# A recurrent attention and a maxout layer in one kernel: units of four batches with four tokens a partition, 32-row tiles and a tabled order in place of units of two batches and a stepped loop

## The chip, the core and the metric

The kernel runs on one core of one Trainium2 chip. The engines of the core run side by side, each with a queue of its own that it works off in order: TensorE (PE; its loads of weights, PEld, are listed apart), VectorE (DVE), ScalarE (ACT), GpSimd (POOL), and SyncE (SP), which here only issues DMA transfers. Matmul results go to PSUM, eight banks of 2 KB a partition; GpSimd does not read PSUM in this kernel. The metric is the device time of one execution in microseconds, lower is better; the median of the runs is given.

## The reference

Two stages in float32. The first is a recurrence with a decay for each channel (4 batches, 8 heads, 768 tokens, head size 48); the second a maxout layer over all 3072 tokens (384 to 1024 and back), whose input row holds the 8 heads of one token side by side.

```python
for t in range(S):
    cur = np.einsum('bhd,bhe->bhde', u[None] * kt, vt)
    y[:, :, t] = np.einsum('bhd,bhde->bhe', rt, state + cur)
    state = wt[:, :, :, None] * state + np.einsum('bhd,bhe->bhde', kt, vt)
...
h1 = x @ w1
h2 = x @ w2
g = np.maximum(h1, h2)
return (g @ w_out).astype(np.float32)
```

## The kernel before

The recurrence is done in chunks of 128 tokens. With P the running product of the decays inside a chunk, the score of token t for an earlier token s is r·P(before t) times k/P(through s); the scores are masked to earlier tokens and multiplied with v ("intra"). The state that comes in adds r·P times S ("carry"), and the token itself adds v times the sum of u·r·k ("bonus"). The state after the chunk is (S + sum of k/P times v) times the whole chunk's P.

*Tiles.* A unit is one chunk of two batches: 256 tokens, 12 units. 64 partitions hold a batch, each with two neighbouring tokens (`i` = 0, 1). `load` (L71) issues eight DMAs a unit (w, k, r, v for two batches), each with pieces of 384 B.

*A unit's work.* `logw` (L167): Ln on ScalarE, the pair's sum on GpSimd. `cumsum` (L194): an fp32 matmul with a triangular matrix gives the sum of the logarithms of all partitions before; VectorE adds the tokens' own. `exps` (L206): Exp of these sums and of their negatives, and a DMA on ScalarE's queue writes the last row to DRAM, from where `decay_load` (L218) fetches it again in the layout of the state. `scale_rk` (L227) multiplies r and k; `transp` (L233) turns them on TensorE (16 transposes) and VectorE copies them out of PSUM. `kv` (L253, 64x64 tiles of the array), `scores` (L284, 48x64 tiles; VectorE masks in one multiply each), `y_inter` (L300: the bonus rows placed by a selection matrix, L308, and the carry, L315), `y_intra` (L319, 64x128 tiles). ScalarE copies y out, `xt` (L335) turns it.

*The maxout layer.* max(h1, h2) = ((h1 + h2) + |h1 - h2|) / 2. So `gate` (L344) makes x @ (w1 - w2), in 24 matmuls of 256 columns, and ScalarE takes Abs; `outp` (L359) adds x @ wc to |.| @ (w_out / 2), where wc = (w1 + w2) @ w_out / 2 is folded once, in `weights` (L143).

*The order.* It is the program's order. `step(a, t, m)` (L376) interleaves three units: the preparation of `a`, the recurrence of `t`, the maxout layer of `m`. Two units go ahead, then comes `weights()`, then ten steps with all three. `load(n + 2)` stands ahead of a step. Loads have four buffers; output DMAs (one for 128 tokens) stand on the same SP queue, between the loads. A DMA waits until the eighth before it has landed, so at most eight are in flight.

Of the kernel before, what the change touches and what calls it, by code (L numbers as in the profile page):

```python
# [33 lines left out]

def _body(tc, r, k, v, w, u, moe_w1, moe_w2, moe_w_out, out):
# [3 lines left out]
    C = 128  # L39
    Q = C // 2  # L40
    NC = S // C
# [6 lines left out]
    NU = NC * B // 2  # L48
# [4 lines left out]
    ldp = tc.alloc_tile_pool(name="ld", bufs=4)  # L53
    wk = tc.alloc_tile_pool(name="wk", bufs=2)
    drp = tc.alloc_tile_pool(name="dr", bufs=3, space=bass.MemoryType.DRAM)
    ps = tc.alloc_tile_pool(name="ps", bufs=1, space=bass.MemoryType.PSUM)

    def wt_(shape, dt, tag, bufs=None):
        return wk.tile(shape, dt, tag=tag, name=tag, bufs=bufs)

    def pt_(shape, dt, tag, bufs=1):
        return ps.tile(shape, dt, tag=tag, name=tag, bufs=bufs)

    def unit(n):
        return n // 2, (n % 2) * 2

    L = {}

    def load(n):  # L71
        c, b0 = unit(n)
        d = {}
        for name, src in (("w", w), ("k", k), ("r", r), ("v", v)):
            t = ldp.tile([P, H, 2, D], F32, tag="l" + name, name="l" + name)
            for b in range(2):
                nc.sync.dma_start(  # L77
                    out=t[b * Q:(b + 1) * Q].rearrange("p h i d -> p h (i d)"),
                    in_=src[b0 + b, :, c * C:(c + 1) * C, :].rearrange(
                        "h (p i) d -> p h (i d)", i=2))  # L80
            d[name] = t
        L[n] = d

    load(0)
    u_b = const.tile([P, HD], F32)
    nc.sync.dma_start(out=u_b, in_=u.rearrange("h d -> (h d)").partition_broadcast(P))
    load(1)
    w1f = const.tile([P, KO, d_ff], F32)
    w2f = const.tile([P, KO, d_ff], F32)
    wof = const.tile([P, FO, HD], F32)  # L90
    nc.sync.dma_start(out=w1f, in_=moe_w1.rearrange("(o p) n -> p o n", p=P))
    nc.sync.dma_start(out=w2f, in_=moe_w2.rearrange("(o p) n -> p o n", p=P))
    nc.sync.dma_start(out=wof, in_=moe_w_out.rearrange("(o p) n -> p o n", p=P))
    load(2)


    triS = const.tile([P, P], F32)
    make_upper_triangular(nc, triS, val=1.0, diag=False)
    triI = const.tile([P, P], F32)
    make_upper_triangular(nc, triI, val=1.0, diag=True)  # L100
    tri2 = const.tile([P, P], F32)
    nc.gpsimd.memset(tri2, 0.0)
    ident = const.tile([P, P], BF16)
    make_identity(nc, ident)
    mask = const.tile([P, 2, 2, Q], F32)
    sel = const.tile([P, 2, 2, Q], BF16)
    nc.gpsimd.memset(sel, 0.0)
    for b in range(2):
        q = slice(b * Q, (b + 1) * Q)
        nc.gpsimd.tensor_copy(tri2[q, q], triS[q, q])  # L110
        for i in range(2):
            nc.gpsimd.tensor_copy(sel[q, i, i, :], ident[q, q])
            for i2 in range(2):
                nc.gpsimd.tensor_copy(mask[q, i, i2, :],
                                      (triI if (i, i2) == (0, 1) else triS)[q, q])

    NRK = 2
    rkn_b = []
    for i in range(NRK):
        t = const.tile([P, 2, 2, H, DP], BF16, name=f"rkn{i}")  # L120
        nc.vector.memset(t, 0.0)
        rkn_b.append(t)
    MZ = [const.tile([P, 2, H, DP], F32, name=f"mz{i}") for i in range(2)]
    for t in MZ:
        nc.gpsimd.memset(t, 0.0)

    S_f = [const.tile([P, 2, NP, D], F32, name=f"Sf{g}") for g in range(2)]
    T_f = [const.tile([P, 2, NP, D], F32, name=f"Tf{g}") for g in range(2)]
    S_b = [const.tile([P, 2, NP, 2 * D], BF16, name=f"Sb{g}") for g in range(2)]
    for g in range(2):  # L130
        nc.vector.memset(S_f[g], 0.0)
        nc.vector.memset(S_b[g], 0.0)
    WL = [const.tile([P, 2, NP], F32, name=f"WL{i}") for i in range(2)]
    for t in WL:
        nc.vector.memset(t, 0.0)

    wd_sb = const.tile([P, KO, d_ff], BF16)
    ws_sb = const.tile([P, KO, d_ff], BF16)
    wo_sb = const.tile([P, FO, HD], BF16)
    wsT_sb = const.tile([P, FO, HD], BF16)  # L140
    wc_sb = const.tile([P, KO, HD], BF16)

    def weights():  # L143
        for ko in range(KO):
            nc.vector.tensor_sub(wd_sb[:, ko, :], w1f[:, ko, :], w2f[:, ko, :])
            nc.vector.tensor_add(ws_sb[:, ko, :], w1f[:, ko, :], w2f[:, ko, :])
        nc.scalar.mul(wo_sb, wof, 0.5)
        for ko in range(KO):
            tp = pt_([P, FO, P], BF16, "tr")
            for fo in range(FO):  # L150
                nc.tensor.transpose(tp[:, fo, :], ws_sb[:, ko, fo * P:(fo + 1) * P], ident)
            nc.vector.tensor_copy(
                wsT_sb.rearrange("p f (k c) -> p k f c", k=KO)[:, ko, :, :], tp)
        for ko in range(KO):
            wc_p = pt_([P, HD], F32, "go", 2)
            for fo in range(FO):
                nc.tensor.matmul(wc_p, wsT_sb[:, fo, ko * P:(ko + 1) * P],
                                 wo_sb[:, fo, :], start=(fo == 0), stop=(fo == FO - 1))
            nc.scalar.copy(wc_sb[:, ko, :], wc_p)


    U = {}

    def byi(t):
        return t.rearrange("p h i d -> p i h d")

    def logw(n):  # L167
        s = U[n] = {}
        s["lw"] = lw = wt_([P, H, 2, D], F32, "lw")
        nc.scalar.activation(lw, L[n]["w"], AF.Ln)  # L170
        s["lp"] = lp = wt_([P, H, D], F32, "lp")
        nc.gpsimd.tensor_add(lp, lw[:, :, 0, :], lw[:, :, 1, :])  # L172

    def bonus_mul(n):
        s = U[n]
        s["vb"] = vb = wt_([P, H, 2, D], BF16, "vb", 3)
        nc.gpsimd.tensor_copy(vb, L[n]["v"])
        s["rku"] = rku = wt_([P, H, 2, D], F32, "rku", 1)
        nc.gpsimd.tensor_mul(rku, L[n]["r"], L[n]["k"])  # L179
        nc.gpsimd.tensor_mul(  # L180
            byi(rku), byi(rku),
            u_b.rearrange("p (h d) -> p h d", h=H).unsqueeze(1).to_broadcast([P, 2, H, D]))

    def bonus_sum(n):
        s = U[n]
        dg = wt_([P, H, 2, 1], F32, "dg")
        nc.vector.reduce_sum(dg, s["rku"], axis=AX.X)  # L187
        s["vd"] = vd = wt_([P, 2, H, D], BF16, "vd", 3)
        nc.gpsimd.tensor_mul(byi_inv(vd), L[n]["v"], dg.to_broadcast([P, H, 2, D]))  # L189

    def byi_inv(t):
        return t.rearrange("p i h d -> p h i d")

    def cumsum(n):  # L194
        s = U[n]
        lw, lp = s["lw"], s["lp"]
        ex = pt_([P, HD], F32, "ex")
        nc.tensor.matmul(ex, tri2, lp.rearrange("p h d -> p (h d)"))  # L198
        s["A"] = A = wt_([P, 2, H, D], F32, "A")
        s["mz"] = mz = MZ[n % 2]  # L200
        exh = ex.rearrange("p (h d) -> p h d", h=H)
        nc.scalar.activation(A[:, 0], exh, AF.Exp)  # L202
        nc.vector.tensor_add(mz[:, 0, :, 0:D], exh, lw[:, :, 0, :])  # L203
        nc.vector.tensor_add(mz[:, 1, :, 0:D], exh, lp)

    def exps(n):  # L206
        s = U[n]
        mz = s["mz"]
        nc.scalar.activation(s["A"][:, 1], mz[:, 0, :, 0:D], AF.Exp)  # L209
        s["iA"] = iA = wt_([P, 2, H, D], F32, "iA", 1)  # L210
        nc.scalar.activation(iA, mz[:, :, :, 0:D], AF.Exp, scale=-1.0)
        c, b0 = unit(n)
        if c == NC - 1:
            return
        s["row"] = row = drp.tile([2, H * DP], F32, tag="row", name="row")
        nc.scalar.dma_start(out=row, in_=mz[Q - 1::Q, 1].rearrange("b h d -> b (h d)"))

    def decay_load(n):  # L218
        c, b0 = unit(n)
        if c == NC - 1:  # L220
            return
        s = U[n]
        s["WL"] = wl = WL[n % 2]
        nc.scalar.dma_start(out=wl.rearrange("d b p -> d (b p)"),
                            in_=s["row"].rearrange("b (p x) -> x (b p)", x=P))

    def scale_rk(n):  # L227
        s = U[n]
        s["rkn"] = rkn = rkn_b[n % NRK]
        nc.vector.tensor_mul(rkn[:, 0, :, :, 0:D], byi(L[n]["r"]), s["A"])  # L230
        nc.vector.tensor_mul(rkn[:, 1, :, :, 0:D], byi(L[n]["k"]), s["iA"])  # L231

    def transp(n, x):  # L233
        s = U[n]
        tp = pt_([P, NP, 2, 2, Q], BF16, "tr")
        for i in range(2):
# [8 lines left out]
    def decay_exp(n):  # L245
        c, b0 = unit(n)
        if c == NC - 1:
            return
# [127 lines left out]
    def step(a, t, m, ahead=True):  # L376
# [10 lines left out]
        if T: kv(t)  # L387
# [64 lines left out]
```

## Time and profile before

| what | us |
|---|---|
| median of 3 runs (226.53 to 227.88) | 227.76 |
| span of the profiled execution | 226.8 |
| TensorE busy | 159.0 |
| VectorE busy | 114.1 |
| GpSimd busy | 113.6 |
| ScalarE busy | 91.7 |
| first gate matmul | 55.9 |
| start of the last output copy on ScalarE | 216.45 |

The profiled execution is known by its span, from its first to its last instruction; the median of the other runs is 0.96 us above that. "Busy" is the time in which at least one instruction of the engine was running; matmuls are pipelined, so their busy time holds latencies. "SPq" is time in which SP issues DMAs, or waits to issue them. A row of a timeline gives the start, the time from the first start to the last end of a group of like instructions, the engine, the line, the tiles and the count.

### The profile page before, as it was taken

What the parts mean: (1) busy time and instruction counts of PE and PEld (TensorE: products, weight loads), DVE (VectorE), ACT (ScalarE), POOL (GpSimd) and SP (SyncE); (2) the same over time, 40 slices, a digit from 0 to 9 for tenths busy, and PEclk for the clock granted to TensorE, in tenths of its full rate; (3) what the DMA queues carried; (4) which work ended last, traced back from release to release, by engine and by line L of the source; (5) the groups of instructions that cost most, each with busy time, mean ns of one, the idle gap of its engine ahead of it and who ended that gap; (6) DMA issues with size and microseconds to landing.
All of it is one profiled execution on the core that took longest, in us unless ns stands there. A gap on an engine that the chain in (4) does not pass through costs nothing.

```text
span 226.8 us, 5085 instructions
## 1 busy us (share of the span) xinstructions
PE 159.0 (70%) x2104; PEld 104.3 (46%) x2104; DVE 114.1 (50%) x135; ACT 91.7 (40%) x159; POOL 113.6 (50%) x118
## 2 busy tenths in 40 slices
PE   0216557195799848898839898378888398988910
PEld 0014444153576634666615656236556156665600
DVE  5166878710969490185840785802858405660000
ACT  2233113303765613464433556035644347344500
POOL 8494750004788828638549179086295494300000
PEclk9999999999999995899976999959999679999975
DMA  6979999990296439539584485385385811111110
GB/s 128 211 113 217 406 356 134 198 152 0 66 150 129 104 104 172 133 76 151 141 163 104 100 169 117 101 158 132 85 143 146 177 49 50 53 52 31 48 42 35
DMA packets 66254, 28.91 MB, mean 127 GB/s; under 512 B 61220, under 2 KB 65444, under 8 KB 66232
## 3 DMA queue, kind: packets, MB, share of 16 engines
q1 hardware_dynamic: 55792, 28.51, 55.0%
q10 hardware_dynamic: 10440, 0.08, 2.7%
q8 instruction: 16, 0.26, 0.5%
q14 instruction: 6, 0.05, 0.1%
HBM read 23.83 MB, written 4.76 MB: 126 GB/s over the span
## 4 chain that ended last, share of the span: by engine, by line
DMA 20%; PE 16%; SPq 8%; ACT 5%; issue 2%; DVE 1%; POOL 0%; ACTq 0%; DVEq 0%
DMA lw<-in_w_dram 20%; PE go L367 6%; SPq L77 6%; PE go L352 3%; PE go L364 3%; SPq L373 2%; ACT gT L356 2%; PE sc L293 1%; PE y L328 1%; ACT xT L342 1%; ACT osb L370 1%; ACT lw L170 1%; DVE kT L243 1%; PE y L315 1%; PE y L308 1%
## 5 line engine op out<-in xcount | busy, mean ns | idle before, releaser
L172 POOL TENSOR_TENSOR lp<-lw 128x384 f32<-128x384 f32 x12 | 12.3, 1022 | 60.5 <-ACT lw L170 39.5
L367 PE MATMUL go<-wo_sb,gT 128*128 128x384 bf16 x192 | 40.8, 362 | 0.0
L352 PE MATMUL go<-xT,wd_sb 128*128 128x256 bf16 x288 | 37.2, 273 | 2.5 <-ACT xT L342 1.5
L296 DVE TENSOR_TENSOR M<-sc,mask 128x1024 bf16<-128x1024 f32 x24 | 29.3, 1221 | 8.4 <-PE sc L293 8.4
L364 PE MATMUL go<-wc_sb,xT 128*128 128x384 bf16 x72 | 19.0, 381 | 18.7 <-ACT gT L356 18.7
L352 PEld LDWEIGHTS <-wd_sb 128*128 128x128 bf16 x288 | 26.9, 98 | 10.3 <-issue 5.5
L243 DVE COPY rT<-tr 128x1024 bf16<-128x1024 bf16 x12 | 8.3, 688 | 45.8 <-PE tr L238 45.8
L356 ACT ACTIVATE gT<-go 128x512 bf16<-128x512 f32 x48 | 27.3, 588 | 5.6 <-PE go L352 5.4
L370 ACT COPY osb<-go 128x384 f32<-128x384 f32 x24 | 11.5, 478 | 43.3 <-PE go L367 43.3
L367 PEld LDWEIGHTS <-gT 128*128 128x128 bf16 x192 | 20.7, 108 | 16.7 <-issue 6.7
L198 PE MATMUL ex<-lp,tri 128*128 128x384 f32 x24 | 12.1, 592 | 19.5 <-POOL lp L172 14.8
L180 POOL TENSOR_TENSOR rku<-rku,u_b 128x768 f32<-128x768 f32 x12 | 22.4, 1863 | 0.9
L179 POOL TENSOR_TENSOR rku<-lr,lk 128x768 f32<-128x768 f32 x12 | 22.4, 1868 | 0.0
L189 POOL TENSOR_TENSOR vd<-lv,dg 128x768 bf16<-128x768 f32 x12 | 17.7, 1474 | 9.1 <-DVE dg L187 8.3
L170 ACT ACTIVATE lw<-lw 128x768 f32<-128x768 f32 x12 | 10.1, 842 | 29.2 <-DMA lw<-in_w_dram 29.2
L203 DVE TENSOR_TENSOR mz<-ex,lw 128x384 f32<-128x384 f32 x12 | 6.7, 557 | 27.9 <-ACT A L202 27.9
L238 PE MATMUL tr<-ident,rkn 128*128 128x128 bf16 x192 | 16.3, 234 | 4.3 <-DVE rkn L230 3.0
L364 PEld LDWEIGHTS <-xT 128*128 128x128 bf16 x72 | 6.5, 105 | 23.0 <-issue 21.0
L238 PEld LDWEIGHTS <-rkn 128*128 128x128 bf16 x192 | 13.6, 105 | 7.0 <-DVE rkn L230 4.4
L231 DVE TENSOR_TENSOR rkn<-lk,iA 128x768 bf16<-128x768 f32 x12 | 16.0, 1333 | 0.0
L230 DVE TENSOR_TENSOR rkn<-lr,A 128x768 bf16<-128x768 f32 x12 | 15.5, 1293 | 0.3 <-ACT A L209 0.2
L333 ACT CAST x<-y 128x768 bf16<-128x768 f32 x12 | 9.6, 798 | 13.1 <-PE y L328 12.9
(56 smaller groups left out, 215.2 us busy)
## 6 DMA issues: line engine op xcount, KB each, us to landing
lw<-in_w_dram SPq DMA_DIRECT2D x24, 192.0 KB
lk<-in_k_dram SPq DMA_DIRECT2D x24, 192.0 KB
lr<-in_r_dram SPq DMA_DIRECT2D x24, 192.0 KB
lv<-in_v_dram SPq DMA_DIRECT2D x24, 192.0 KB
out_dram<-osb SPq DMA_DIRECT2D x24, 192.0 KB
w1f<-in_moe_w_dram SPq DMA_DIRECT2D x1, 1536.0 KB
w2f<-in_moe_w_dram SPq DMA_DIRECT2D x1, 1536.0 KB
wof<-in_moe_w_out_dram SPq DMA_DIRECT2D x1, 1536.0 KB
```

Of the source, the lines that this page charges most:

```text
L179: nc.gpsimd.tensor_mul(rku, L[n]["r"], L[n]["k"])
L180: nc.gpsimd.tensor_mul(byi(rku), byi(rku), u_b.rearrange("p (h d) -> p h d", h=H).unsqueeze(1).to_broadcast([P, 2, H, D]))
L189: nc.gpsimd.tensor_mul(byi_inv(vd), L[n]["v"], dg.to_broadcast([P, H, 2, D]))
L230: nc.vector.tensor_mul(rkn[:, 0, :, :, 0:D], byi(L[n]["r"]), s["A"])
L231: nc.vector.tensor_mul(rkn[:, 1, :, :, 0:D], byi(L[n]["k"]), s["iA"])
L238: nc.tensor.transpose(tp[:, p, :, i, :], s["rkn"][:, x, i, 2 * p:2 * p + 2, :].rearrange("s r d -> s (r d)"), ident)
L296: nc.vector.tensor_mul(M.rearrange("s e p t -> s (e p) t"), sc.rearrange("s e p t -> s (e p) t"), mask[:, i].rearrange("s i q -> s (i q)") ...
L352: nc.tensor.matmul(g[:, f, :], wd_sb[:, ko, fo * P:(fo + 1) * P], s["xT"][:, ko].rearrange("p j t -> p (j t)"), start=(f == 0 and ko == 0) ...
L356: nc.scalar.activation(s["gT"][:, 2 * j:2 * j + 2].rearrange("p f j t -> p f (j t)"), g, AF.Abs)
L364: nc.tensor.matmul(o, s["xT"][:, ko, b, :], wc_sb[:, ko, :], start=(ko == 0), stop=False)
L367: nc.tensor.matmul(o, s["gT"][:, fo, b, :], wo_sb[:, fo, :], start=False, stop=(fo == FO - 1))
L370: nc.scalar.copy(osb, o)
```

## The change

All of the body is new. What it does, part by part:

- *Units.* A unit is 128 tokens of all four batches: 512 tokens, 6 units. 32 partitions hold a batch, each with four neighbouring tokens. A unit has 16 loads with pieces of 768 B; two buffers each.
- *Paired logarithms.* GpSimd multiplies the decays of tokens 0 and 1, and of 2 and 3 (`wp`); Ln and Exp are taken of these products only. The token inside the pair is put right by multiplying r of the second token with w of the first (`rw`) and k of the first with w of the second (`kw`).
- *32-row tiles.* kv uses 32x64 tiles of the array, the scores 48x32, intra 32x128, the bonus 32x32, the carry 128x32. There are 3990 matmuls where there were 2092.
- *Diagonal bonus blocks.* `dd` spreads the bonus sums onto the diagonals of 32x32 blocks, and `yd` multiplies them with v (128 matmuls a unit), in place of the products on GpSimd and the selection matmuls.
- *Relu maxout.* max(h1, h2) = h2 + relu(h1 - h2): wc = w2 @ w_out, and Relu in place of Abs, on ScalarE for 38 of 48 tiles, on VectorE for ten. The gate has 24 matmuls of 512 columns for 512 tokens.
- *PSUM.* Two banks for transposes and the prefix sum ("A"), two for gate, output and folding ("G"), two pairs ("Y") that kv, scores and y share.
- *DMA queues.* All DMAs stand on SP. The decay row and its fetch move there from ScalarE's queue; 128 tokens of output go out in four DMAs of 32 rows instead of one.
- *Order.* A table lists each step with its engine (`@a` ScalarE, `@d` VectorE, `@p` GpSimd); it is the order of every engine. The masks (64 copies of 32x32 blocks, and 4 for a small identity) and the weights' preparation stand in the same table, among the first unit.

The core of the diff; only new lines are shown, the ones they replace stand in the kernel above:

```diff
+UNITS = (4, 4, 4, 4, 4, 4)
+ORDER = """
+consts zeros load.0.w load.0.k load.0.r wp.0@p u load.0.v ln.0 lq.0@p ex.0 wload.1.0 wload.0.0 mz.0
+e0.0 wload.1.1 rk.0.0@d e1.0 wload.0.1 ie.0 row.0 ru.0.0@d rk.0.1@p wload.1.2 vb.0.0@p kw.0@d
+ru.0.1@p w2cast.0@a vb.0.1@d w2turn.0 wdiff.0@d scale.0.1.0@p w2take.0@a w2cast.1@a dg.0 wload.0.2
+woload.0 rw.0@p tr.0.1.0 w2turn.1 wl.0 te.0.1.0@a wdiff.1@d w2take.1@a w2cast.2@a dd.0 woload.1
+woload.2 wdiff.2@p w2turn.2 wocast.0@a scale.0.1.1@d scale.0.0.0@d tr.0.1.1 we.0 woload.3 load.1.w
...
+gt.1.6 gt.1.7 rl.1.6@a dd.2 yi.2 kw.3@p ya.2.1 sb.2.1@a ya.2.0 rl.1.7@d ya.2.2 ya.2.3 sb.2.0@d yd.2
...
+rl.5.4@a rl.5.5@a gt.5.6 gt.5.7 rl.5.6@a op.4.2 rl.5.7@d op.5.0 oe.4.2@d os.4.2 op.5.1 oe.5.0@a
+os.5.0 op.5.2 oe.5.1@a os.5.1 op.5.3 oe.5.2@a os.5.2 oe.5.3@a os.5.3
+""".split()
...
+        for j in range(4):
+            for i in range(4):
+                for q in range(B):
+                    p = slice(q * G, (q + 1) * G)
+                    nc.gpsimd.tensor_copy(mask[p, j, i, :], (triI if j < i else triB)[p, p])
...
+    def load(s, name):
+        src = {"w": w, "k": k, "r": r, "v": v}[name]
+        t = wt_([P, H * 4 * D], F32, "l" + name, 2)
+        t = t[:, 0:H * s.ni * D].rearrange("p (h i d) -> p h i d", h=H, i=s.ni)
+        for b in range(B):
+            nc.sync.dma_start(
+                out=t[b * G:(b + 1) * G].rearrange("p h i d -> p h (i d)"),
+                in_=src[b, :, s.t0:s.t0 + G * s.ni, :].rearrange("h (p i) d -> p h (i d)", i=s.ni))
...
+    def wp(s, e):
+        s.lg = wt_([P, 2, HD], F32, "lg", 2)
+        mul(e, s.lg[:, 0:s.A].rearrange("p a (h d) -> p a h d", h=H),
+                             split(s.w, 0), split(s.w, 1))
...
+    def rw(s, e):
+        mul(e, split(s.r, 1), split(s.r, 1), split(s.w, 0))
...
+    def kv(s):
+        s.kvp = [pair(), pair()]
+        for i in range(s.ni):
+            for p in range(NP):
+                for e in range(2):
+                    for q in range(B):
+                        h = 2 * p + e
+                        g = slice(q * G, (q + 1) * G)
+                        nc.tensor.matmul(
+                            s.kvp[q // 2][e * DP:(e + 1) * DP, q % 2, p * D:(p + 1) * D],
+                            s.kp[g, i, h, :], s.vb[g, h, i, :],
...
+    def sc(s, j):
+        t = pair()
...
+        for p in range(NP):
+            for q in range(B):
+                for e in range(2):
+                    d = slice(e * DP, e * DP + D)
+                    nc.tensor.matmul(
+                        t[q * G:(q + 1) * G, e, p * w_:(p + 1) * w_].rearrange("k (i g) -> k i g", g=G),
+                        s.kT[d, j, p, q, :],
+                        s.rT[d, 0:s.ni, p, q, :], skip_group_check=True)
...
+    def yd(s):
+        for h in range(H):
+            for j in range(s.ni):
+                for q in range(B):
+                    g = slice(q * G, (q + 1) * G)
+                    o = yrows(s, q).start + j * G
+                    nc.tensor.matmul(s.y[q // 2][o:o + G, q % 2, h * D:(h + 1) * D],
+                                     s.D[g, j, h, :], s.vb[g, h, j, :], start=False,
+                                     stop=(h == H - 1 and j == s.ni - 1), skip_group_check=True)
...
+    def rl(s, f, e):
...
+        if e == "a":
+            nc.scalar.activation(o, i, AF.Relu)
+        else:
+            nc.vector.tensor_scalar_max(o, i, 0.0)
...
+    def os(s, b):
+        t = getattr(s, f"os{b}")
+        for x in range(4):
+            q, i = (b, x) if s.ni == 4 else (2 * b + x // 2, x % 2)
+            dst = out[q * S + s.t0:q * S + s.t0 + G * s.ni, :].rearrange("(g i) n -> g i n", i=s.ni)
+            nc.sync.dma_start(out=dst[:, i, :], in_=t[x * G:(x + 1) * G])
```

In the table `wp`, `ln`, `lq`, `ex`, `mz`, `e0`, `e1`, `ie` are the logarithms, sums and exponentials, `row`, `wl`, `we` the decay row, `rk`, `ru`, `dg`, `dd` the bonus, `scale`, `tr`, `te` the scaled r and k and their turning, `kv`, `st`, `sm`, `sb` the state, `sc`, `mk` scores and masks, `yi`, `ya`, `yd` carry, intra and bonus, `xe`, `xt`, `xc` y on its way to the layer, `gt`, `rl`, `op`, `oe`, `os` gate, Relu, output, its copy and its DMAs. The first number is the unit.

## The prediction

> **What bounds the kernel now.** I read the page's totals first, then busy time in stretches, the chain of waits, the waiting lists, and last the timelines of TensorE, GpSimd and the SP queue.
>
> ```profile
> PE 159.0 (70%) x2104; PEld 104.3 (46%) x2104; DVE 114.1 (50%) x135; ACT 91.7 (40%) x159; POOL 113.6 (50%) x118
> ...
> DMA packets 66254, 28.91 MB, mean 127 GB/s; under 512 B 61220, under 2 KB 65444, under 8 KB 66232
> ```
>
> No engine is full over the whole span. The stretches (PE, PEld, DVE, ACT, POOL busy, clock, DMA share, GB/s) say why:
>
> ```profile
> 0.00:10.00 10.00, 1.65 (x2) 0.50 (x2) 3.37 (x8) 2.12 (x2) 7.34 (x29) 1.00 0.94 161
> ...
> 60.00:70.00 10.00, 9.58 (x133) 6.54 (x133) 7.24 (x10) 6.31 (x13) 8.00 (x7) 1.00 0.72 122
> ...
> 100.00:120.00 20.00, 14.73 (x199) 9.42 (x196) 12.22 (x14) 8.32 (x17) 13.11 (x13) 0.90 0.73 150
> ```
>
> Where inputs are there (60 to 70), TensorE is 96% busy; later 74%, at a lower granted clock. In the first 10 us full DMA engines moved 161 GB/s of 384 B pieces (the input loads); from 20 to 30, with the weights' 4 KB rows among them, 362. The chain of waits repeats this from unit to unit:
>
> ```profile
> 104.57 2.47 SPq L77
> ...
> 107.08 8.65 DMA lw<-in_w_dram
> ```
>
> The waiting lists (total, times, longest) show who pays: Ln waits for w, the Abs behind it on ScalarE is late, and so is TensorE.
>
> ```profile
> ACT lw L170 <- DMA lw<-in_w_dram: 29.2, 9, 5.6
> PE go L364 <- ACT gT L356: 18.7, 7, 4.7
> ```
>
> The timelines give three parts: the start until the first gate matmul (55.9), the body until the last output copy ends (216.45 + 0.48 = 216.9), and 9.9 us to the span's end at 226.8. The prices are here too:
>
> ```profile
> 55.87 2.32 PE L352 MATMUL go<-xT,wd_sb 128*128 128x256 bf16 x18
> ...
> 66.88 0.44 PE L266 MATMUL y<-vb,rkn 64*64 64x48 bf16 x32
> 67.43 0.42 PE L293 MATMUL sc<-rT,kT 48*64 48x128 bf16 x16
> 67.78 1.48 PE L352 MATMUL go<-xT,wd_sb 128*128 128x256 bf16 x12
> ...
> 72.21 0.57 PE L328 MATMUL y<-vb,M 64*128 64x48 bf16 x32
> 72.71 0.66 PE L364 MATMUL go<-wc_sb,xT 128*128 128x384 bf16 x3
> ```
>
> ```profile
> 216.45 0.48 ACT L370 COPY osb<-go 128x384 f32<-128x384 f32 x1 [1.31 <-PE go L367]
> ```
>
> ```profile
> 3.54 0.41 POOL L114 COPY mask<-triS 64x64 f32<-64x64 f32 x2
> ```
>
> ```profile
> 130.86 1.31 SPq L77 DMA_DIRECT2D lr<-in_r_dram  x2
> ```
>
> A small matmul is priced by its group: its length less one matmul (0.19 us, the last one's latency) over the number less one. That is 8 ns for the 64x64 tiles, 12 ns for 64x128 and for the scores. The change of tile shape adds 0.13 to 0.3 us before the next group starts (32 of L266 take 0.25, the next group starts 0.55 after the first).
>
> **TensorE's work.** Per 512 tokens before: 2 x (gate 24 x 0.118, output 22 x 0.163, transposes 0.9, prefix sum 0.72, kv 0.55, scores 2 x 0.35, bonus 0.43, carry 0.36, intra 0.50, turning x 0.34; all from one group's start to the next in the same timeline, 64 to 76) = 21.9 us. After, a unit has: gate 24 matmuls of 512 columns, half as many loads of weights, 5.2 (24 x 0.217, twice the 108 ns of six gate matmuls in 0.65 us); output unchanged 7.2; transposes 1.8; one prefix sum 0.72; turning 0.7; kv 128 x 8 ns + 0.3 = 1.3; scores 4 x (32 x 12 ns + 0.16) = 2.2; intra 4 x (32 x 12 + 0.13) = 2.0; bonus blocks 128 x 10 ns + 0.13 = 1.4; carry 64 x 11 + 0.13 = 0.85 (96 columns took 45 ns, four column tiles side by side). Sum 23.4. So 3,264 small matmuls take the place of 1,216, and cost 7.75 us a unit against 5.1; gate and prefix sum give 1.2 back. No row shows a 32-row tile. Bounds: a pace of 8 ns for all (9 us less over the run), and of 15.6 ns, at which L328's 32 reach the next group (0.50 us, taken as the pace itself: 17 more). I take the rows nearest in shape, which lie between. Twice the instructions have to be fetched: the page's two instruction queues use 0.5% and 0.1% of the DMA engines, so I price that at nothing; if it fails, it shows in the small groups, as rival 3.
> The Trainium skill speaks against this. In "TensorE: Matmul & The Clock Gate", section "Wait — 56ns, not 53.3ns?", it says that matmuls never start closer than about 25 ns. By it the 3,264 would take 82 us, not 44, and the sum below would be 241. The row of 32 matmuls in 0.44 us contradicts it for tiles that sit side by side.
>
> **The start.** GpSimd writes 68 mask blocks of 32x32 (4 + 64) ahead of all else. Copies start 0.176 us apart; 2.4 + 12.0 + 0.5, and 1.7 for zeros: free at 16.6, where it did its first logarithm sum at 7.28 before. Then one after another: product of pairs 1.87, Ln 0.84, pair sum 1.02, cold prefix sum 1.65, Exp 0.49, add of 768 in PSUM 0.96, Exp 0.52 and 0.84, hand-overs: 25.4. VectorE's three products (1.3 each beside a busy GpSimd) end at 27.8, GpSimd's scaling 1.47 at 29.3, r*w 1.87 at 31.2, its share of the weight difference (2.4) at 34.9. That frees the buffer that the last piece of w_out waits for on SP, and behind that piece stands load 1: issued at 35.6, w landed at 40. Product, Ln and sum: 43.9; prefix sum 1, ahead of unit 0's y on TensorE, 45. The four masked score tiles end near 47 (1.22 each, two PSUM pairs), y 3.4, copies and turning 2.8: first gate matmul at **53** against 55.9. Folding the weights (19 us of its own before, 36 to 55) now lies beside this. Bounds 46 (products at 0.94, no buffer wait) and 62 (products at 2.56, the dearest row).
>
> **The body.** TensorE's work from there is 6 x 23.4 - 2.2 (no kv in the last unit, no carry in the first) - 10.9 done before = **127 us**; the other engines' sums over the same list are 82 (VectorE; masks 24 x 1.22 unchanged), 73 (ScalarE; Relu in the form of the Abs, 38 x 0.588, ten more on VectorE) and 72 (GpSimd). VectorE's 82 has 0.94 for a product; at 1.3 beside GpSimd it is 90, still covered by 127. The kernel before has 12 x 10.9 less some 10 done by 55.9 = 121 in its 161, so 40 go to waits and slow clock.
> SP is next. It issues 96 loads (0.66 each), 96 output pieces where there were 24 (0.6), and the decay row's ten small ones, which move from ScalarE's queue (a decay row can be fetched again only when it has landed, and the loads behind it on SP wait with it). From load 1 to load 5's v it has 80 x 0.66 + 28 x 0.6 + 6 x 0.4 = 72 us: 35.6 + 72 = 108, in order, with at most eight in flight. Pieces are 768 B, so I estimate 250 GB/s (between 161 and 362): 6 us for eight, the last lands at 114. Waits inside that queue (outputs for their copies, a row for its sum, lanes) I put at 0 to 11, and take 5. The copies of unit 5's v on VectorE and ScalarE come 60 us into TensorE's list, at 113; all masks, gates' relu and output copies of these engines are queued behind. So 7 us of wait, and 5 for the new in-order waits (kv, scores and y share two PSUM pairs; prices 1.22 for a mask, 0.56 for a state sum): **12**, bounds 0 and 40.
> By the Trainium skill's "DMA: Bandwidth & Descriptors", Specifications, pieces from 512 B up go at line rate; then these 7 us would be near 2 and the sum 198. No row here shows 768 B.
>
> **The end.** One output piece became four: 9.9 + 2 x 0.6 = **11**.
>
> Sum: 53 + 127 + 12 + 11 = 203 for the span. The median of the runs (227.76) is 0.96 above the profiled span, so **204**. Pairs halve Ln and Exp per token (ScalarE 93 in all as against 92 with more copies); covered as long as TensorE is the longer.
>
> **Rivals.**
> 1. *SP's queue hides.* Waits 0 to 2, as in 60 to 70 now: 53 + 127 + 1 + 11 + 1 = **193**. For it: 96% there. Against it: SP is issuing for nearly all of the time that TensorE works.
> 2. *The waits only change name.* The listed order meets one late item (decay row, v, a mask) after another, and loses 33 where I put 12: **225**, about no change. For it: every engine is in order, the PSUM pairs serve three uses. Against: units overlap, and gate and output matmuls stand between.
> 3. *32-row tiles cost more.* The 44 us of small groups are about 10 ns a matmul without the changes of shape. At 19 ns, 3,264 x 9 = 29 more: **233**, slower. Place: kv, scores, intra, bonus, carry. It decides from some 17 ns, where the 24 us of gain are gone. For it: the dearest pace above is 15.6. Against it: 8 ns with 64x64 tiles, and more tiles lie side by side now.
>
> **How the numbers follow.** The forecast 0.42 (197 to 212 by itself), rival 1 0.27, rival 2 0.18, rival 3 0.13. Within 1% (225.5 to 230.0) is about what a measurement of this kernel can't tell from no change. Faster: 0.42 + 0.27 + 0.10 of rival 2 = 0.79; same 0.04 + 0.02 of rivals 2 and 3 = 0.06; slower 0.04 + 0.11 = 0.15. The range 186 to 228 leaves out the lower part of rival 1 (0.06), most of rival 3 and the top of 2 (0.13).
>
> **What would show it.** GpSimd's first product at 16.6; first gate matmul at 53; 128 kv matmuls in some 1.2 us; SP issuing almost without a gap until about 115; TensorE's idle time from the first gate on at 12. Wrong if the small groups take twice their price, if the first gate comes after 62, or if VectorE waits longer for loads than TensorE's list allows.

## The result, and the profile after

The changed kernel takes 237.56 us (235.73 to 241.16, five runs) against 226.90 (226.53 to 227.88, five runs) for the kernel before on the same chip: ratio 1.0424, 95% interval 1.0371 to 1.0478. It is slower; forecast were 204. The profiled execution is one of the two slow ones (240.14 us, span 238.1; the spans of the three others are 233.7 to 235.6), so its times are up to 2% long, and where medians below are of all runs, ratios leave slow ones out (without them the medians are 236.43 for after, 229.64 for e2, 211.69 for e13, 213.38 for e14 and 214.16 for e17; for e15 and e17 one run of the kernel before is left).

The engines' row, the transfers and the instruction queues on the page of the kernel after, then the windows that stood above for the kernel before:

```profile
PE 157.5 (66%) x3996; PEld 96.9 (41%) x3996; DVE 135.9 (57%) x126; ACT 90.1 (38%) x136; POOL 129.2 (54%) x147
...
DMA packets 43214, 29.17 MB, mean 122 GB/s; under 512 B 13588, under 2 KB 42388, under 8 KB 43176
...
q8 instruction: 31, 0.51, 1.0%
...
PE 52%; issue 18%; DVE 8%; POOL 8%; DMA 5%; SPq 4%; ACT 2%; DVEq 0%; POOLq 0%
```
```profile
0.00:10.00 10.00, 0.00 (x0) 0.00 (x0) 3.43 (x4) 1.28 (x1) 7.89 (x42) 1.00 0.87 170
60.00:70.00 10.00, 3.05 (x129) 2.31 (x128) 1.56 (x2) 3.45 (x5) 5.63 (x4) 0.57 1.14 216
100.00:120.00 20.00, 15.35 (x512) 9.40 (x512) 14.26 (x15) 10.29 (x16) 12.79 (x8) 0.77 0.83 155
```

TensorE is as busy as before (157.5 against 159.0), but in a span that is 11 us longer, and where it was busy for 9.58 of the 10 us from 60 to 70 it is now for 3.05, at a granted clock of 0.57; this stretch now lies ahead of the first gate matmul. The packets are a third fewer (43,214 against 66,254). 18% of the chain is "issue": time in which an engine waited for nothing that the profile shows. The waits say where most of it sits (what waited, what for, total, times, longest):

```profile
ACT gT L524 <- PE G L515: 19.1, 20, 4.1
...
PEld L467 <- issue: 17.4, 6, 6.0
PE Y L467 <- issue: 16.7, 6, 5.9
...
PE Y L457 <- issue: 9.0, 4, 3.7
...
PE Y L408 <- issue: 2.5, 2, 2.3
```

It is TensorE, inside its runs of small matmuls. TensorE's timeline around the first gate matmul, and in unit 2 (in brackets the idle time ahead of a group and its releaser):

```profile
55.54 0.38 PE L457 MATMUL Y<-vb,M 32*128 32x48 bf16 x32
55.84 1.02 PE L467 MATMUL Y<-vb,D 32*32 32x48 bf16 x107
62.78 0.29 PE L467 MATMUL Y<-vb,D 32*32 32x48 bf16 x21 [5.91 <-issue]
63.00 1.15 PE L457 MATMUL Y<-vb,M 32*128 32x48 bf16 x96
65.03 1.42 PE L489 MATMUL A<-identb,x 128*128 128x128 bf16 x11 [0.89 <-ACT x L139]
69.52 0.26 PE L489 MATMUL A<-identb,x 128*128 128x128 bf16 x1 [3.07 <-issue]
70.44 1.89 PE L515 MATMUL G<-xT,wd_sb 128*128 128x512 bf16 x4 [0.65 <-DVE xT L139]
...
119.11 0.83 PE L457 MATMUL Y<-vb,M 32*128 32x48 bf16 x83
123.59 0.66 PE L457 MATMUL Y<-vb,M 32*128 32x48 bf16 x45 [3.66 <-issue]
124.18 0.87 PE L467 MATMUL Y<-vb,D 32*32 32x48 bf16 x83
127.32 0.55 PE L467 MATMUL Y<-vb,D 32*32 32x48 bf16 x45 [2.27 <-issue]
```

Count the matmuls between two stops: 21 + 96 + 11 = 128, and 45 + 83 = 128. Numbered from the first, every stop comes after a matmul whose number leaves 95 over 128: 479, 607, 863, 1119 and so on, 16 stops of 33.2 us in sum. 128 matmuls with their 128 loads of weights are 256 instructions. The page's instruction queue q8 has 31 packets of 16,384 B, and 2 x 3,996 / 256 = 31.2; before it had 16, and 2 x 2,104 / 256 = 16.4. In the kernel before TensorE stops inside a group only where a semaphore is awaited. And each of the 16 stops ends 1.3 to 1.7 us after a packet of q8 has landed; for the stop that ends at 62.78 it landed at 61.34.

The groups themselves run as priced. 128 kv matmuls, the last output copy, a load on SP and the mask copies of the kernel after:

```profile
79.20 1.23 PE L380 MATMUL Y<-vb,kp 32*64 32x48 bf16 x128
```
```profile
233.29 0.48 ACT L139 COPY osb<-G 128x384 f32<-128x384 f32 x1 [1.26 <-DMA out_dram<-osb]
```
```profile
143.77 3.04 SPq L238 DMA_DIRECT2D lv<-in_v_dram  x4
```
```profile
11.19 2.89 POOL L156 COPY mask<-triB 32x32 f32<-32x32 f32 x12
...
20.93 1.80 POOL L143 TENSOR_TENSOR lg<-lw 128x768 f32<-128x768 f32 x1
```

The parts of the span, as the prediction cut it. "Stops" are TensorE's pauses of more than 0.1 us that await no semaphore (all lie inside a line's group, but for one of 3.7 us in e12); "pairs" are matmuls, each with its load of weights. The runs are told below.

| kernel | median us | ratio to before (95%) | pairs | stops | first gate | body | end |
|---|---|---|---|---|---|---|---|
| before | 226.90 | | 2104 | 0 | 55.9 | 161.1 | 9.9 |
| forecast | 204 | | | 0 | 53 | 139 | 11 |
| after | 237.56 | 1.042 (1.037 to 1.048) | 3996 | 33.2 | 70.4 | 163.3 | 4.3 |
| e1 bonus in 16 | 215.96 | 0.958 (0.950 to 0.967) | 3324 | 13.3 | 66.9 | 142.3 | 4.6 |
| e2 masks on VectorE | 230.26 | 1.025 (1.012 to 1.037) | 3996 | 27.4 | 65.3 | 156.2 | 4.8 |
| e3 fewer pairs | 216.50 | 0.962 (0.953 to 0.970) | 2764 | 4.7 | 64.4 | 146.0 | 4.3 |
| e6 = e1 + e2 | 210.82 | 0.928 (0.922 to 0.934) | 3324 | 15.8 | 64.1 | 142.0 | 4.3 |
| e7 = e3 + e2 | 210.60 | 0.932 (0.923 to 0.941) | 2764 | 4.4 | 59.6 | 144.1 | 4.6 |
| e8 order alone | 235.91 | 1.037 (1.032 to 1.042) | 3996 | 23.4 | 70.7 | 159.2 | 4.3 |
| e9 = e6, output in one DMA | 216.78 | 0.954 (0.950 to 0.959) | 3324 | 16.4 | 63.1 | 144.1 | 7.9 |
| e10 = e9, r and v reused | 211.10 | 0.928 (0.923 to 0.933) | 3324 | 10.0 | 62.5 | 138.6 | 7.8 |
| e12 = e6, carry in 16 | 210.97 | 0.932 (0.926 to 0.938) | 3084 | 14.0 | 63.6 | 141.0 | 4.6 |
| e13 = e6, loads later | 213.37 | 0.935 (0.924 to 0.946) | 3324 | 12.3 | 60.0 | 144.5 | 4.3 |
| e17 = e6, scaling on VectorE | 214.65 | 0.953 (0.932 to 0.974) | 3324 | 15.0 | 64.4 | 143.5 | 4.4 |

### The profile page after: what moved, and what is told of

Read it like the earlier page. It is cut to its first block, busy times and chain, and to the rows that moved or that the text cites. A ratio compares the mean times of both kernels' runs of the same rounds, so it can differ in the third digit from the quotient of the medians.

```text
span 238.1 us, 8876 instructions
## 1 busy us (share of the span) xinstructions
PE 157.5 (66%) x3996; PEld 96.9 (41%) x3996; DVE 135.9 (57%) x126; ACT 90.1 (38%) x136; POOL 129.2 (54%) x147
## 2 busy tenths in 40 slices
DMA packets 43214, 29.17 MB, mean 122 GB/s; under 512 B 13588, under 2 KB 42388, under 8 KB 43176
## 4 chain that ended last, share of the span: by engine, by line
PE 52%; issue 18%; DVE 8%; POOL 8%; DMA 5%; SPq 4%; ACT 2%; DVEq 0%; POOLq 0%
PE G L515 14%; PE G L535 10%; POOL mask L156 5%; PE G L532 4%; PE A L349 4%; PE Y L457 4%; PE Y L408 3%; PE Y L467 3%; PE A L489 3%; SPq L548 3%; DMA lv<-in_v_dram 2%; PE A L259 2%; PE G L209 2%; DMA lk<-in_k_dram 2%; SPq L238 2%
## 5 line engine op out<-in xcount | busy, mean ns | idle before, releaser
L515 PE MATMUL G<-xT,wd_sb 128*128 128x512 bf16 x144 | 40.6, 415 | 1.1 <-DVE xT L139 0.7
L535 PE MATMUL G<-wo_sb,gT 128*128 128x384 bf16 x192 | 37.5, 342 | 0.0
L416 DVE TENSOR_TENSOR M<-Y,mask 128x1024 bf16<-128x1024 f32 x24 | 28.7, 1219 | 9.4 <-PE Y L408 9.4
L524 ACT ACTIVATE gT<-G 128x512 bf16<-128x512 f32 x38 | 22.5, 599 | 19.8 <-PE G L515 19.1
L515 PEld LDWEIGHTS <-wd_sb 128*128 128x128 bf16 x144 | 13.8, 105 | 22.3 <-issue 8.5
L143 POOL TENSOR_TENSOR rp<-lr,E 128x768 bf16<-128x768 f32 x9 | 20.0, 2240 | 5.1 <-DVE lr L143 5.1
L143 POOL TENSOR_TENSOR kp<-lk,iE 128x768 bf16<-128x768 f32 x8 | 15.5, 1945 | 3.4 <-DVE lk L143 2.8
L532 PE MATMUL G<-wc_sb,xT 128*128 128x384 bf16 x72 | 17.2, 351 | 0.0
L314 DVE TENSOR_TENSOR D<-id,dg 128x1024 bf16<-128x1024 bf16 x6 | 14.0, 2336 | 0.1
L408 PE MATMUL Y<-rT,kT 48*32 48x128 bf16 x768 | 11.0, 234 | 4.4 <-issue 2.5
L143 POOL TENSOR_TENSOR S_f<-T_f,W 128x384 f32<-128x384 f32 x6 | 5.0, 828 | 16.4 <-DVE T_f L388 16.4
```

Source lines behind the costliest of these rows:

```text
L143: (nc.vector if e == "d" else nc.gpsimd).tensor_mul(o, a, b)
L314: nc.vector.tensor_mul(s.D[:, 0:s.ni], id32.unsqueeze(1).unsqueeze(1).to_broadcast([P, s.ni, H, G]), s.dg[:, :, 0:s.ni].rearrange("p h i o ...
L408: nc.tensor.matmul(t[q * G:(q + 1) * G, e, p * w_:(p + 1) * w_].rearrange("k (i g) -> k i g", g=G), s.kT[d, j, p, q, :], s.rT[d, 0:s.ni, p ...
L416: nc.vector.tensor_mul(t, getattr(s, f"sc{j}")[:, :, 0:NP * w_].rearrange("s e (p t) -> s e p t", p=NP), mask[:, j, 0:s.ni].rearrange("s i ...
L515: nc.tensor.matmul(t[:, 0:s.nb * P].rearrange("c (b t) -> c b t", t=P), wd_sb[:, ko, f * P:(f + 1) * P], xs(s, ko), start=(ko == 0), stop= ...
L524: nc.scalar.activation(o, i, AF.Relu)
```

## The experiments

Theory A: TensorE's instructions come in blocks of 256 (one packet), a block takes a fixed few microseconds to come, longer behind loads, and whatever runs through 128 pairs faster than that must stop. Its rivals: B, a 32-row tile costs more wherever it stands; C, the waits between engines and queues. 

**e5, the pace alone.** Three runs of 1,024 small pairs, each after some large matmuls: 32x32 tiles, 64x64 tiles, and 32x32 tiles while loads land. All else is left out.

> Only the pace of small matmuls, by itself: the kernel leaves out the whole computation and writes zeros. Three runs of 1024 pairs, with 48 matmuls of 512 columns ahead of, between and behind them: 32x32 tiles with idle DMA engines, 64x64 tiles with idle DMA engines, 32x32 tiles while 80 input loads (768 B pieces) are landing. Theory A: all three stop every 128 pairs, with the same spacing for both tile shapes: some 3.5 us for 128 pairs with idle DMA engines (28 us for 1024), 5 to 6 us with loads (40 to 48 us), and between two stops 8 ns a pair. Theory B: no stops; 64x64 at 8 ns (8 us for 1024) and 32x32 slower than that, with or without loads.

TensorE's timeline, a few groups of each run:

```profile
23.32 1.25 PE L55 MATMUL y<-x 32*32 32x48 bf16 x128 [2.26 <-issue]
27.05 1.24 PE L55 MATMUL y<-x 32*32 32x48 bf16 x128 [2.48 <-issue]
30.50 1.24 PE L55 MATMUL y<-x 32*32 32x48 bf16 x128 [2.21 <-issue]
...
69.18 1.91 PE L65 MATMUL y<-x 64*64 64x48 bf16 x128 [1.55 <-issue]
72.63 1.91 PE L65 MATMUL y<-x 64*64 64x48 bf16 x128 [1.55 <-issue]
...
103.04 1.25 PE L55 MATMUL y<-x 32*32 32x48 bf16 x128 [4.98 <-issue]
110.06 1.24 PE L55 MATMUL y<-x 32*32 32x48 bf16 x128 [5.77 <-issue]
```

128 pairs, then a stop, again and again. A block of 32x32 tiles takes 1.24 us, less 0.19 for the last one's latency and over 127: 8.3 ns a pair, inside the prediction's bounds. But blocks start 3.45 to 3.73 us apart, with 64x64 tiles too: 27 to 29 ns a pair over a long run, whatever the tile. With loads landing they start 5.7 to 7.0 us apart. The first stop of a run comes after 175 to 255 pairs: that much was there when the run began. For the pace A holds, and B falls.

**e1, the bonus in 16 matmuls.** 672 pairs fewer; VectorE multiplies v by the bonus sums instead of spreading these over diagonals (2.60 us a unit instead of 2.34).

```diff
-        for h in range(H):
-            for j in range(s.ni):
+        for j in range(4):
...
-                                     s.D[g, j, h, :], s.vb[g, h, j, :], start=False,
+                                 s.vd[g, j].rearrange("g h d -> g (h d)"), start=False,
```

> The bonus alone: 16 matmuls a unit of 384 columns (a 32x32 identity times v already scaled with the bonus sums) in place of 128 of 48 columns. The array streams the same columns, 672 pairs of weight load and matmul fall away in all. Theory A (TensorE runs out of instructions: it stops without a wait after each 128 pairs, whenever such a run of small pairs is shorter than the fetch of the next 256 instructions): the 16.7 us that TensorE stands inside the bonus groups go, a part of it comes back in the groups beside them; idle time inside groups from 33 us to some 18, time from 236 to 223-228. Theory B (small 32-row tiles are slow in themselves): the groups' own busy time is 8 us and the columns stay, so at most 3 us: 233 or more. Theory C (late start and crowded GpSimd and VectorE): the product on VectorE has half again as many elements, so no gain, 235 to 240.

215.96 us, some 21 less than after, where 672 pairs at 8 to 12 ns would be 5 to 8. The stops fall by 19.9 us, to 13.3. In the body alone (142.3 us, 163.3 in after) TensorE's stops fall by 15.5 us and its busy time by 8.2, and its other idle time rises by 2.6. A's sign is right and its size was too small; B (233 or more) and C (235 to 240) fail.

**e2, the masks on VectorE.**

```diff
-                    nc.gpsimd.tensor_copy(mask[p, j, i, :], (triI if j < i else triB)[p, p])
+                    nc.vector.tensor_copy(mask[p, j, i, :], (triI if j < i else triB)[p, p])
```

> The 64 mask copies go from GpSimd to VectorE, which is idle until 27 us; nothing else changes. Theory C (the start): the first prefix sum comes near 12 instead of 24.7, the first gate matmul some 9 to 12 us earlier than 70.4, and so does the end: 225 to 228. Theory A (instruction fetch): the start gains the same at first, but the stops inside groups stay (some 33 us in all) and loads and weights are then waited for: the end comes 4 to 8 us earlier, 229 to 232.

230.26 us, as A had it (229 to 232), and not C (225 to 228). GpSimd's timeline:

```profile
6.86 1.81 POOL L143 TENSOR_TENSOR lg<-lw 128x768 f32<-128x768 f32 x1 [1.50 <-DMA lw<-in_w_dram]
```

The first product starts at 6.9 us, not 20.9, and waits for its load; the first gate matmul gains only 5.2 of these 14, because loads, the weights' transfers and VectorE's own work then fill the chain of the start.

**e3, fewer pairs still.** Besides e1 the carry in 16 matmuls of 128x128 and the state's product in 64 of 32x128 a unit; the state sum on VectorE then takes four additions a unit instead of two.

> As the bonus alone, and also the carry in 16 matmuls of 128x128 tiles instead of 64 of 128x32 (the turned r is stored with its four tokens side by side), and kv in 64 of 32x128 instead of 128 of 32x64 (two heads at once; the two off-diagonal quarters are left aside). Pairs fall from 576 to 352 a unit, columns streamed by the array do not fall. VectorE gets four state sums a unit in place of two. Theory A: idle time inside groups falls to 8-14 us, time to 213-220. Theory B: carry and kv use wider tiles but each pair streams as many columns, so 230 to 236. Theory C: 234 to 240.

216.50 us: inside A's range, with 8.6 us of stops less than e1, and yet no gain on e1. **e6** (e1 with e2) tells whether the two large terms add.

> The bonus in 16 matmuls a unit and the 64 mask copies on VectorE together. If TensorE's instruction fetch and the late start are two separate terms, their gains add: 215.96 - (237.56 - 230.26) = 208.7, so 207 to 212 us, with the first prefix sum near 10.7 us as in the run with the masks alone. Rival, the loads set the middle: in the run with the bonus alone v of unit 5 landed at 142.6 us, and taking 320 more pairs a unit away gained nothing (216.5); if the 24 loads are what runs through the middle whenever the stops are gone, an earlier start brings at most 2 us: 213 to 217.

210.82 us: they do, within some 2 us. It is the fastest whole form here, with e7 and e12 its equals: 7% under the kernel before. **e7** puts e3 and e2 together, and **e12** adds to e6 only the carry in 16 matmuls, for which the turned r is stored in another order.

> The masks on VectorE with the fewest pairs: bonus and carry in 16 matmuls each and the state's product in 64 of 32x128, for which each unit's two state sums on VectorE become four (553 ns each). Without the masks' move this was 216.5 us against 215.96 with the bonus alone, although 320 pairs a unit fewer and 9 us less of stops. If that is because VectorE, at 150 us busy, then set the time, it is no better than the run with the bonus in 16 and the masks on VectorE here either: 210 to 214. If the stops still cost what they last, 203 to 208.

> As the run with the bonus in 16 matmuls and the masks on VectorE (210.8 us, stops of 16 us), and the carried state's part in 16 matmuls of 128x128 a unit rather than 64 of 128x32: 48 pairs fewer in each of five units, and no instruction more on any engine. If the stops still set the time, 240 of 3,324 pairs less take 1 to 3 us: 208 to 210. If VectorE and GpSimd set it (154 and 120 us busy there), nothing: 210 to 212.5.

210.60 and 210.97: with 560 and 240 pairs fewer than e6 in the whole run (not 320 a unit, as the expectations of e6 and e7 have it), and stops of 4.4 and 14.0 us instead of 15.8, nothing moves. The body's stretch in after, e1, e6 and e7, with TensorE's busy time first, shows what became of the stops:

```profile
70.44:233.77 163.33, 135.69 (x3388) 82.02 (x3388) 99.62 (x94) 70.11 (x110) 81.69 (x46) 0.88 0.47 92
66.87:209.21 142.34, 127.52 (x2828) 76.39 (x2828) 101.16 (x94) 70.13 (x112) 84.78 (x47) 0.91 0.57 111
64.14:206.12 141.98, 127.19 (x2828) 75.35 (x2828) 101.04 (x94) 70.27 (x112) 84.59 (x46) 0.93 0.56 109
59.55:203.69 144.14, 125.24 (x2332) 74.86 (x2332) 110.89 (x102) 69.90 (x111) 92.02 (x49) 0.94 0.58 112
```

Of what is left of each, stops take 24.2, 8.7, 8.9 and 3.1 us, and 3.5, 6.1, 5.9 and 15.8 us are other idle time. In e7 TensorE stops less and waits more, for VectorE most of all (9.8 of the 15.8 us). A microsecond of stop is not a microsecond of time.

**e8, the order alone.** Same instructions; gate and output chains of the unit before are put between the small runs of units 2 to 4.

```diff
...
-gt.1.6 gt.1.7 rl.1.6@a dd.2 yi.2 kw.3@p ya.2.1 sb.2.1@a ya.2.0 rl.1.7@d ya.2.2 ya.2.3 sb.2.0@d yd.2
-scale.3.1.0@p load.5.w ru.3.1@d op.1.1 xe.2.0@a wl.3 xe.2.1@a dg.3 wp.4@p xt.2.0 oe.1.1@a op.1.0
+mk.2.3 rl.1.5@a dd.2 yi.2 gt.1.6 kw.3@p ya.2.1 rl.1.6@a gt.1.7 sb.2.1@a ya.2.0 rl.1.7@d ya.2.2
+ya.2.3 op.1.1 sb.2.0@d yd.2 scale.3.1.0@p load.5.w ru.3.1@d xe.2.0@a wl.3 xe.2.1@a dg.3 wp.4@p
...
```

> The kernel after with six TensorE items moved to later or earlier places in its order and nothing else: two gate chains and three output chains of the unit before come between the runs of small matmuls of units 2, 3 and 4. Same instructions, same count. Theory A (TensorE is fed 256 instructions at a time, and large matmuls give the fetch time to run ahead): the stops of units 2 to 4, 14.6 us in the profile after (1.38, 3.66, 2.27, 1.69, 1.57, 0.21, 1.63, 2.16), fall below 7, and the time falls by 4 to 9 us: 228 to 234. Rival B (each 32-row load and matmul costs its time wherever it stands): the stops do not change in sum and the time stays within 1% of 237.6. Rival C (the chains moved made room for waits on VectorE's masks): the stops fall, but waits with a semaphore take their place and the time is 236 to 242.

The stops of units 2 to 4 fall from 14.6 to 4.8 us (one inside a gate group, 0.29 and 0.68 us, left aside), as A says and B forbids. But the time, 235.91, can't be told from after's: A's 228 to 234 fails, and what happened is nearest to C. Outside the stops TensorE idles for 8.9 us of the body, where it was 3.5 in after. Unit 2 in the timeline of e8:

```profile
117.04 0.27 PE L445 MATMUL Y<-Sb,rT 128*32 128x96 bf16 x8
...
121.39 0.51 PE L458 MATMUL Y<-vb,M 32*128 32x48 bf16 x45 [0.35 <-issue]
121.83 0.66 PE L533 MATMUL G<-wc_sb,xT 128*128 128x384 bf16 x3
...
126.76 0.60 PE L468 MATMUL Y<-vb,D 32*32 32x48 bf16 x56 [2.30 <-issue]
128.28 0.51 PE L490 MATMUL A<-identb,x 128*128 128x128 bf16 x6 [0.93 <-ACT x L140]
```

The stops of unit 2 are down from 7.3 to 2.7 us. But from the first matmul of y to the end of the last copy of x it is 11.9 us here and was 12.7 in after, and in unit 3 it is 16.0 and was 12.6: the stop has become useful work, and y is hardly sooner done. y holds both PSUM pairs from its first matmul to the last copy of x, and kv and scores of the next unit need them. Summed over the units that time is 66.1 us in after, 69.3 in e8, 48.0 in e1, 45.5 in e6. After to e1 it falls by 18.1 us, about as much as the total. In these four the time goes with y's hold on the pairs, but the other runs don't follow it: 39.5 us in e3, which is no faster than e1, and 50.1 in e15, which is no slower than e6. So it isn't shown that a stop costs by this hold, and a kernel with a pair of its own for y wasn't tried.

**e9, one DMA for an output tile**, as the kernel before had it.

```diff
-        for x in range(4):
...
-            nc.sync.dma_start(out=dst[:, i, :], in_=t[x * G:(x + 1) * G])
+        nc.sync.dma_start(out=dst, in_=t)
```

> As the run with the bonus in 16 matmuls and the masks on VectorE, and each 128x384 output tile leaves in one DMA (as before the change) rather than in four, so 24 output issues on SP's queue and not 96. If SP's queue holds the loads back (96 issues at 0.45 us are 43 us, and SP waits 31 us on the output copies, which stays), the loads of units 4 and 5 land up to 5 us earlier and the time falls by 2 to 6 us against that run: 203 to 210. If the DMA engines set the loads' pace (their share is over 90% from 44 to 100 us in the run with the bonus alone), or if the wait on the output copies and not the issues does, nothing changes: within 1% of that run. The end of the kernel may change by up to 2 us either way: one DMA of 192 KB is spread over the same engines, but lands as a whole.

216.78 us, 6 slower than e6, outside both expectations. The end grows by 3.6 us and the body by 2. An output transfer in the chain of e9, and then the four that e6 issues at the same time, 124.6 to 125.9 us (the landing of three of them is known):

```profile
124.70 9.14 DMA out_dram<-osb
```
```profile
DMA to landing us min/median/max: 4.5/4.8/5.2
```

Among loads one transfer of 192 KB landed 9.1 us after its issue, and quarters of it 4.5 to 5.2 us after theirs; over the whole of e6 the median of a quarter is 1.6. What 72 issues fewer on SP may have brought is less than what this cost.

**e10, eight loads left out** (units 2 to 5 use the r and v of two units before).

> As the run with one DMA an output tile, and r and v are loaded for units 0 and 1 alone: units 2 to 5 work on the tiles of two units before, so 8 of the 24 loads (6.3 of 18.9 MB) are left out and the output is not the reference's. If the loads set the middle, it gets shorter by a good part of 8 x 3.7 us (768 KB at about 205 GB/s): 15 us or more less than that run, 188 to 198. If the products on VectorE and GpSimd (2.0 to 2.5 us each, contended) set it, the time stays within 3 us of that run.

211.10, 5.7 us under e9: less than if loads set the middle, more than if products did. The stops fell by 6.4 us, so the gain may well be fetches that come sooner with fewer loads about; this isn't shown.

**e13, two loads later**, and **e14**, the same with the carry in 16 matmuls.

> As the run with the bonus in 16 matmuls and the masks on VectorE (210.8 us), and the loads of w and k of unit 2 stand later in the order, behind the small matmuls of unit 0, so that SP issues w of unit 2 about 5 us later. If TensorE's fetches queue on the DMA engines behind the loads, the first long stop (6.12 us at matmul 479, with two loads outstanding) shrinks to 2 to 4 us, as in the run of bare pairs with idle DMA engines (2.2 to 2.5 us against 4.4 to 5.8), and the time falls by 1 to 4 us: 207 to 210. If the length of a stop has nothing to do with the loads, it stays at 5 to 6.5 us and the time stays or rises by the loads' delay: 210 to 214.

> The bonus and the carried state in 16 matmuls each, the masks on VectorE and the later loads of unit 2, together. If both edits work by shorter stops: 205 to 209. If the loads' delay or the products set the middle by then: 210 to 213.

The long first stop shrinks from 6.12 to 3.82 us, as expected, and the first gate comes 4.1 us sooner (60.0). But the time, 210.64 to 215.09 us, can't be told from e6's, and e14, 213.98 (ratio 0.943, 0.934 to 0.952), lies above both of its expectations. In e13's profile the body is 2.5 us longer than in e6; that the later loads do this was argued beforehand and isn't shown.

**e16, products alone; e15, 12 products left out** (the factor u of the bonus); **e17, the scalings on VectorE.** These ask what holds e6, e7 and e12 at 211.

> Products of 128x768 fp32 by themselves (the whole computation is left out; the output is zeros): 8 on VectorE alone, 8 on GpSimd alone, then 16 on VectorE beside 8 on GpSimd with all inputs from SBUF, then the same with one of VectorE's inputs from PSUM. If the two engines exclude each other when both read SBUF: alone 0.95 and 1.81 us; side by side VectorE's that wait take about 1.81 + 0.95 less the start, 2.4 to 2.8 us, GpSimd's 1.8 to 2.8; with an input from PSUM 0.95 and 1.81 again. If they share bandwidth instead, all of those side by side lengthen evenly, with PSUM too. If the long ones in the trace have another cause (DMA traffic), side by side is as alone.

Groups of e16 by form (L56 and L59: an engine alone; L62 beside L64 and L69: both):

```profile
L62 DVE TENSOR_TENSOR t<-t,t 128x768 f32<-128x768 f32 x15 | 36.6, 2439 | 0.5
L69 POOL TENSOR_TENSOR t<-t,t 128x768 f32<-128x768 f32 x8 | 19.3, 2410 | 0.5
L64 POOL TENSOR_TENSOR t<-t,t 128x768 f32<-128x768 f32 x8 | 18.6, 2321 | 0.5
...
L59 POOL TENSOR_TENSOR t<-t,t 128x768 f32<-128x768 f32 x7 | 12.6, 1799 | 0.6
L56 DVE TENSOR_TENSOR t<-t,t 128x768 f32<-128x768 f32 x8 | 7.6, 950 | 0.2
```

Side by side a product on each engine takes 2.3 to 2.4 us, and 16 on each went by in 39.6, so 2.48 a pair; one after the other a pair would take 0.95 + 1.80 = 2.75. Working at once saves some 0.3 us of a pair. The Trainium skill's "SBUF — State Buffer", section "Who interferes with whom", says that a VectorE instruction with two SBUF inputs and a GpSimd instruction that reads SBUF exclude each other; these rows come close to that. VectorE's products with an input from PSUM ran after GpSimd had finished, so that side by side stays unmeasured here; the masks multiplied from PSUM took 1.22 us on average before and after.

> As the run with the bonus in 16 matmuls and the masks on VectorE (210.8 us), with the 12 products by the bonus vector u left out (7 on GpSimd, 5 on VectorE; the output then lacks the factor u of the bonus). If the products of the two engines set the time by then, 12 of some 70 less give 5 to 12 us: 199 to 206. If TensorE with its remaining stops does: 209 to 212.5.

> As the run with the bonus in 16 matmuls and the masks on VectorE, and the scalings of units 1 to 5 that stand on GpSimd moved to VectorE at the same place of the order; nothing is left out. Each takes 0.95 us there alone instead of 1.81. If the two engines exclude each other and their sum sets the time, the sum falls by some 12 us and the time by 2 to 6: 205 to 209. If each engine's own queue sets it, VectorE (154 us busy) gets later and the time rises to 211 to 217.

e15: 208.78, 2.0 under e6, which lies inside the measurement's scatter (ratio 0.930, 0.909 to 0.952), though the instructions of VectorE and GpSimd last 24 us less in sum. e17: 214.65, as the second of its expectations had it; no gain, and the queue's order on VectorE may be what costs. The products' sum doesn't set 211 by itself. What does stays open. TensorE's own work fills most of it: in e6 it is busy for 127.2 of the body's 142.0 us, and for 37.6 of the 38 us from 168 to 206, and the first gate comes at 64.

## Why the prediction was wrong

1. *The step that failed* is one sentence: "Twice the instructions have to be fetched: the page's two instruction queues use 0.5% and 0.1% of the DMA engines, so I price that at nothing". The share was read rightly (it went to 1.0%) and says nothing: blocks come one by one, about 3.5 us apart at the least, and a block of small pairs is used up in 1.2. TensorE stopped for 33.2 us, of which 9.0 lie ahead of the first gate; taking 672 pairs out gave back some 21, about 8 of them the pairs' own time. Rival 3 ended near the right time (233) by luck, with another mechanism: inside a block a pair takes 8 ns, as "TensorE's work" had it, and kv took 1.23 us where 1.2 was said. The Trainium skill's rule of 25 ns ("TensorE: Matmul & The Clock Gate", section "Wait — 56ns, not 53.3ns?") was weighed and left on the ground of a row of 32 matmuls. The row was right, and too short: over a long run it is 27 to 29 ns, by fetches, not by a spacing of matmuls. The page of the skill that bears on it was not weighed: "Runtime: NRT & Kernel Launch", section "Instruction fetch mechanics", gives the blocks of 256 instructions, as the stops show them, and calls the cost of crossing from one to the next "mostly hidden". For small tiles it is not: the 32x32 runs of e5 with idle DMA engines stop for 2.2 to 2.5 us a block. The same section lets TensorE hold 2,048 instructions and then speaks of two cache lines of 256; in e5 the first stop of a run came after 350 to 510 of the run's, which fits the second.
2. *The start*, 53 forecast, 70.4 measured, above its upper bound of 62. Two stops make 9.0. A mask copy took 0.24 us (2.89 for 12), not 0.176, so GpSimd was free at 20.9, not 16.6: 4.3. The rest, 4.1, fits products that cost 1.8 to 2.5 us beside GpSimd where 1.3 was taken. This split is arithmetic and not shown: in e2 GpSimd was free 14 us sooner, and the gate came only 5.2 sooner. The working has a slip too: 31.2 and 2.4 are 33.6, not 34.9.
3. *The body*, 139 forecast, 163.3 measured. TensorE was busy for 135.7 us where 127 was said, stopped for 24.2 where nothing was, and idled otherwise for 3.5 where 12 were: the waits that SP's queue was to cause hardly came. What makes up the 8.7 us of work above the price stays open; the mean granted clock of this stretch was 0.88. It isn't the scores, though their 12 ns was read off wrongly (it takes 0.24 us off their group, not the 0.19 named): 32 of them took 0.42 us, 6 ns each. In e1 and e6 the body is 142.3 and 142.0, near the forecast, but this is partly luck: the 127 holds 8.4 us for bonus blocks that these two don't have, and more than half of their 15 us of idle time are stops. VectorE's and GpSimd's durations in after sum to 142 and 131 us where the shortest of each kind would give 114 and 117.
4. *SP and the loads.* v of unit 5 was awaited until 151.9, not 114; the loads follow the late body, so this is mostly a consequence. With fewer issues on SP (e9) the body was no shorter. Pieces of 768 B did not go at a higher rate: a packet took 62.7 ns on average in after, one of 384 B before 31.4, so the 512 B of the Trainium skill's "DMA: Bandwidth & Descriptors", Specifications, make no step here.
5. *The end*, 11 forecast, 4.3 measured: the four small output transfers land sooner than one large one (e9: 7.9).

e6, which isn't quite the kernel that was forecast, comes to 210.8, against 204: in its profile the start makes +11, the body +3 and the end -7, so a part of the nearness is errors that cancel.

## What to carry to other kernels

Count TensorE's instructions by blocks of 256 and merge small matmuls, which paid here (e1); putting large ones between them took away stops, but no time (e8). With less than some 28 ns of work a pair, TensorE stops once a run outlasts what was fetched ahead (175 to 255 pairs in e5), and longer while loads land. In a trace such a stop has no releaser ("issue") and comes a multiple of 128 matmuls after the one before; what it costs depends on what would have waited otherwise (e3, e7, e8). A product on GpSimd beside one on VectorE, both with all inputs in SBUF, is mostly borrowed time.

## What the runs showed of the hardware that was not expected

- A block of 256 TensorE instructions is one 16,384 B packet; in e5 blocks follow each other 3.45 to 3.73 us apart with idle DMA engines, and 5.7 to 7.0 us while loads land.
- A product of 128x768 takes 0.95 us on VectorE and 1.80 on GpSimd alone, 2.44 and 2.32 to 2.41 side by side.
- Among loads a 128x384 output tile in one transfer landed after 9.1 us, and quarters issued at the same time after 4.5 to 5.2. At the end of the kernel one transfer takes 7.9 us from the last copy on, four take 4.3.
